# SyncE's loads and stores in a fused linear-attention and mixture-of-experts kernel, issued in program order

## The chip, the cores and the metric

The kernel runs on one core of a Trainium2 chip. A core has five engines with a queue of instructions each: TensorE (PE in the profile; its weight loads are PEld), VectorE (DVE), ScalarE (ACT), GpSimd (POOL) and SyncE (SP). SyncE does no arithmetic here: it issues the DMAs, one after the other. An instruction that waits for a semaphore holds up whatever stands behind it in its own queue.

The metric is the device time of one launch in microseconds (us). A time given for a kernel is the median of several runs. A profile is one further execution with its own time.

## The reference

Attention with an exponential feature map on 8 batches, 8 heads, 576 positions and 64 channels gives 4608 rows of 512. A mixture of experts with 8 experts then works on those rows that a gate lets through.

```python
def phi(x):
    proj = np.einsum('bhsd,df->bhsf', x, w_phi)
    proj = proj - np.max(np.abs(proj), axis=-1, keepdims=True)
    return np.concatenate([np.exp(proj), np.exp(-proj)], axis=-1)
q_p, k_p = (phi(q), phi(k))
kv = np.einsum('bhsf,bhsd->bhfd', k_p, v)
z = np.sum(k_p, axis=2)
num = np.einsum('bhsf,bhfd->bhsd', q_p, kv)
den = np.einsum('bhsf,bhf->bhs', q_p, z)[..., None] + 1e-06
x = (num / den)                      # as rows of 512
...
do_compute = x @ w_skip > 0
logits = xc @ w_gate                 # xc: the rows let through
e_idx = np.argmax(logits, axis=1)
...
h = np.maximum(xc[mask] @ w1[e], 0.0)
y[mask] = gate_w[mask, None] * (h @ w2[e])
out[do_compute] = xc + y
```

## The kernel before

**Units and steps.** Attention is cut into 16 units of keys (k) and 16 units of queries (q), each four heads of one batch: unit 2b is the first half of batch b's heads, unit 2b+1 the second. A unit has five items, i = 0 to 4, where item 0 holds the last 64 positions. The loop at L690 runs over 92 steps, numbered t in the code. Unit j of k has its items at steps 5j to 5j+4, and unit j of q six steps later (CFG "off"). At each step the stages work on items of different age (CFG "lag"): the transposition into xT or xTt at once (st_t, L264, on VectorE: L275 for item 0, L277 for items 1 and 2 together and for 3 and 4 together), the projection one step later (st_proj, L280: TensorE L289, VectorE L294 and L296), the exponentials three steps later, the products with v or with the stored state four steps later (st_use_k L346, st_use_q L420).

**What SyncE has to do in attention.** All the DMAs below are on its one queue, and these are the steps at which the program writes them down:

- raw k of unit j+1 (st_load, L243, four DMAs): step 5j. A tile "raw" has four buffers, two for k and two for q in turn, so this load can start when items 3 and 4 of k unit j-1 are transposed, at step 5j-2.
- raw q of unit j (L243, four DMAs): step 5j+1; then v of unit j (st_loadv, L253, four DMAs, two buffers): step 5j+1; then the last positions of v (st_loadvt, L262, four small DMAs, "vt"): step 5j+3.
- three stores for each batch b, kept in the list "later" and written down at the head of their step. store_half (L471, with L473 when b is odd) puts half of the rows into the scratch tensor xrows at step 16+10b; its data are ready two steps before. store_rows (L532, with L534) puts the other half there at step 21+10b, once post (L481) has worked out gate values. rest (L598, with L603 when b is odd) writes the rows to the output at step 27+10b.

Two small loads of gate weights (L115, L116) come at step 6.

**Who sets the order.** The program only writes the instructions down. A scheduler, part of the language, plans the run with its own idea of durations and puts the instructions of each engine in a fixed order; it inserts the semaphores. It prefers what was written down first, but moves an instruction ahead of others that are not ready in its plan. From step 8 to step 78 TensorE is exempt (CFG "man"): there its instructions keep the order of the program. SyncE and the other engines have the scheduler's order everywhere.

**After attention.** Two slots for the busiest experts are picked early (pick, L614) so that their weights (load_chunk, L161: SyncE L170 and L173, ScalarE L174, VectorE or GpSimd L175) can be loaded near the end of attention. Then come the expert phases (mm1, mm2), with rows gathered and results scattered by GpSimd, and a loop for overflow (L1063) that does not run here.

Of the kernel before, what the change touches and what calls it, by code (L numbers as in the profile page):

```python
# [24 lines left out]
def kernel(  # L25
# [88 lines left out]
    def setup_aug():  # L114
        nc.sync.dma_start(out=wgs[:, :, 0:E], in_=w_gate.rearrange("(g p) e -> p g e", p=P))  # L115
        nc.sync.dma_start(out=wgs[:, :, E:E + 1], in_=w_skip.rearrange("(g p o) -> p g o", p=P, o=1))  # L116
        nc.gpsimd.memset(aug, 0.0)
        for hd in range(2):
            r = slice(hd * D, (hd + 1) * D)
            c = hd * NA1  # L120
            for g in range(NP2):
                nc.gpsimd.tensor_copy(out=aug[r, g, c:c + D], in_=ident[r, hd * D:(hd + 1) * D])
            nc.gpsimd.tensor_copy(out=aug[r, :, c + D:c + NA1], in_=wgs[r])

    def setup():
        nc.gpsimd.memset(ones_b, 1.0)
        nc.gpsimd.memset(ones_f, 1.0)
        nc.gpsimd.memset(Stot, 0.0)
        nc.gpsimd.affine_select(
            out=tri, in_=ones_b, pattern=[[1, P]], base=-1, channel_multiplier=-1,  # L130
            compare_op=ALU.is_ge, fill=0.0,
        )
        nc.gpsimd.iota(iota_p, pattern=[[1, P]], base=0, channel_multiplier=0, allow_small_or_imprecise_dtypes=True)
        nc.gpsimd.iota(desc, pattern=[[-1, E]], base=E, channel_multiplier=0, allow_small_or_imprecise_dtypes=True)
        nc.gpsimd.memset(ones_b, 1.0)
        NB2 = B // 2
        kt_i = const.tile([P, 2, NT], I32, name="kt_i")
        kv_ = kt_i.rearrange("p c (b t) -> p c b t", t=9)
        nc.gpsimd.iota(kv_[:, 0, :, 0:8], pattern=[[2 * S, NB2], [512, 2], [1, 4]], base=0, channel_multiplier=4)
        nc.gpsimd.iota(kv_[:, 0, :, 8:9], pattern=[[2 * S, NB2], [1, 1]], base=1024, channel_multiplier=1)  # L140
        for q4 in range(4):
            r = slice(q4 * 32, q4 * 32 + 32)
            nc.gpsimd.iota(
                kv_[r, 1, :, 0:8], pattern=[[2 * S, NB2], [S, 2], [1, 4]], base=4 * q4, channel_multiplier=18)
            nc.gpsimd.iota(
                kv_[r, 1, :, 8:9], pattern=[[2 * S, NB2], [1, 1]], base=(q4 // 2) * S + 16 + q4 % 2, channel_multiplier=18)
        h_i = const.tile([P, 2, NT], I32, name="h_i")
        nc.vector.tensor_scalar(out=h_i[:, 1], in0=kt_i[:, 0], scalar1=127, scalar2=None, op0=ALU.bitwise_and)
        nc.vector.tensor_tensor(out=h_i[:, 0], in0=kt_i[:, 0], in1=h_i[:, 1], op=ALU.subtract)
        nc.vector.tensor_scalar(out=h_i[:, 1], in0=h_i[:, 1], scalar1=1.0, scalar2=None, op0=ALU.add)  # L150
        nc.vector.tensor_copy(out=sid, in_=kt_i[:, 1])
        nc.gpsimd.memset(ft[:, NS2:NSL, 1:2], 0)
        nc.gpsimd.memset(ft[:, NS2:NSL, 3:4], int(BIG))
        nc.vector.tensor_copy(out=ids.rearrange("p t c -> p c t"), in_=h_i)
# [48 lines left out]
    with ExitStack() as actx:  # L203
# [45 lines left out]
        def st_loadv(u):  # L249
            u.v = ld.tile([P, 4, 4 * D], F32, tag="v", name="v")  # L250
            u.vt = vts[u.g % 2]
            for q4 in range(4):
                nc.sync.dma_start(  # L253
                    out=u.v[q4 * 32:q4 * 32 + 32].rearrange("p h (t c) -> p h t c", c=D),
                    in_=vv[u.g][:, :, 4 * q4:4 * q4 + 4, :],
                )

        def st_loadvt(u):
            for pr in range(2):
                for q2 in range(2):  # L260
                    r = pr * 64 + q2 * 32
                    nc.sync.dma_start(out=u.vt[r:r + 32, pr], in_=vv[u.g][:, 2 * pr:2 * pr + 2, 16 + q2, :])  # L262
# [403 lines left out]
        def run_stage(lag, f):  # L666
            for items, us, off in streams:
                s = now[0] - off - lag
                if 0 <= s < n:
                    f(*items[s])  # L670
# [7 lines left out]
        def f_t():  # L678
            for items, us, off in streams:
                s = now[0] - off  # L680
                if s == CFG["ql"]:
                    st_load(us[0])
                if 0 <= s < n:
                    u, i = items[s]
                    st_t(u, i)
                    if i == 0 and s // 5 + 1 < len(us):
                        st_load(us[s // 5 + 1])

        man = None
        for t in range(n + OFF + LA):  # L690
            if CFG["man"] and t == CFG["man"][0]:
                man = ExitStack()
                man.enter_context(tc.manual_schedule(engines={mybir.EngineType.PE}))
            if CFG["man"] and t == CFG["man"][1]:
                man.close()
            now[0] = t
            for w, f in [x for x in later if x[0] <= t]:
                later.remove((w, f))
                f()
            for c in CFG["order"]:  # L700
                if c == "Z":
                    run_stage(LZ, st_z)
                elif c == "A":
                    run_stage(LA, st_aug)
                elif c == "U":
                    run_stage(LU, f_use)
                elif c == "E":
                    run_stage(LE, f_exp)
                elif c == "P":
                    run_stage(LP, st_proj)  # L710
                else:
                    f_t()
            run_stage(LU - 3, lambda u, i: st_loadv(u) if (i == 0 and u.kind == "k") else None)
            run_stage(CFG["vtl"], lambda u, i: st_loadvt(u) if (i == 0 and u.kind == "k") else None)
            if t == CFG["at"]:
                setup_aug()
            if t == 1:
                setup()


    pools = {}
# [378 lines left out]
```

## Time and profile before

| | |
|---|---|
| median of 3 runs (lowest, highest) | 742.93 us (741.94, 747.6) |
| the profiled execution's own time | 747.26 us |
| span from its first to its last instruction | 745.5 us |
| busy over the span: TensorE, VectorE, ScalarE, GpSimd | 616.0, 536.2, 337.8, 352.7 us |
| mean DMA rate over the span | 169 GB/s |

The trace divides into a start, in which the first units are loaded (to about 60 us), a steady part of attention (60 to 380 us), its end (380 to 446 us) and the experts (446 to 738 us). In a row of the timeline stand the start, the length, the engine, the line, the operation, what it writes and reads, the shapes, how many were merged, and in brackets how long the engine sat idle before and what ended that. "SPq" is SyncE's queue: its rows are issues of DMAs, not transfers. In the row of a group, the number behind the bar is the busy time, then the mean in ns, then the engine's idle time just before those instructions and what ended it.

### The profile page before, as it was taken

How to read it: one execution, taken by the hardware profiler on the slowest of the kernel's cores; microseconds unless marked ns; L12 is line 12 of the kernel's file. 1: busy time of each engine (PE TensorE's matmuls, PEld its weight loads, DVE VectorE, ACT ScalarE, POOL GpSimd, SP SyncE). 2: the span in 40 equal slices, each digit the busy share in tenths (PEclk: the TensorE clock that was granted, in tenths of full speed). 3: DMA queues.
4: the chain of work that ended last, by engine and by line, in shares of the span. 5: the costliest groups of instructions: out<-in, count | busy, mean ns of one | idle time of the engine just before them, and what ended most of it. 6: DMA issues, size and time to landing. Idle time of an engine off the chain costs nothing. (4 is left out here: it accounts for less than half of the span.)

```text
span 745.5 us, 16745 instructions
## 1 busy us (share of the span) xinstructions
PE 616.0 (83%) x6333; PEld 506.2 (68%) x6333; DVE 536.2 (72%) x1203; ACT 337.8 (45%) x649; POOL 352.7 (47%) x293
## 2 busy tenths in 40 slices
PE   2468879779888888898799969199989898998994
PEld 1246667657666666676577758188778787987893
DVE  3446579678677885786799769967997568558840
ACT  1224345346345543453454444314667554656520
POOL 3344336245436344362556435735576355555611
PEclk9769999989899988999899988699999899999998
DMA  9985765685487466556532746618788478786500
GB/s 192 199 172 118 163 153 154 151 205 151 102 219 172 116 190 155 149 152 149 151 96 53 211 121 206 204 39 265 224 276 269 144 251 260 235 258 210 188 16 26
DMA packets 82450, 126.03 MB, mean 169 GB/s; under 512 B 12865, under 2 KB 54977, under 8 KB 82368
## 3 DMA queue, kind: packets, MB, share of 16 engines
q1 hardware_dynamic: 79008, 115.43, 58.0%
q0 software_dynamic: 3200, 9.45, 3.9%
q8 instruction: 52, 0.85, 0.5%
q14 instruction: 30, 0.25, 0.1%
q10 hardware_dynamic: 160, 0.07, 0.1%
HBM read 101.68 MB, written 24.02 MB: 169 GB/s over the span
## 5 line engine op out<-in xcount | busy, mean ns | idle before, releaser
L321 POOL TENSOR_TENSOR z<-ek 128x512 f32<-128x512 f32 x64 | 81.3, 1272 | 176.1 <-ACT ek L313 116.9
L175 POOL TENSOR_TENSOR w<-wraw_c,w 128x1024 fp32r<-128x1024 f32 x45 | 108.9, 2435 | 77.7 <-ACT w L174 77.5
L289 PE MATMUL ps_P<-wp,xT 64*128 64x128 f32 x1024 | 91.1, 310 | 61.6 <-DVE u L296 48.2
L289 PEld LDWEIGHTS ps_P<-wp,xT 64*128 64x128 f32 x1024 | 73.1, 205 | 78.9 <-issue 50.9
L174 ACT ACTIVATE w<-wraw_c 128x1024 fp32r<-128x1024 f32 x96 | 100.5, 1057 | 51.2 <-DMA wraw_c<-in_moe_w_dram 39.0
L294 DVE TENSOR_REDUCE m<-ps_P 128x4 f32<-128x512 f32 (+1 forms) x160 | 98.6, 624 | 9.7 <-PE ps_P L289 9.6
L454 PEld LDWEIGHTS ps_O<-kva,eq 128*64 128x64 f32 x2048 | 83.3, 150 | 22.8 <-issue 8.9
L296 DVE TENSOR_TENSOR u<-ps_P,m 128x512 f32<-128x512 f32 (+1 forms) x160 | 97.0, 617 | 2.1
L454 PE MATMUL ps_O<-kva,eq 128*64 128x74 f32 x2048 | 86.9, 243 | 7.5 <-DVE acc L593 5.3
L175 DVE TENSOR_TENSOR w<-wraw_c,w 128x1024 fp32r<-128x1024 f32 x51 | 70.8, 1398 | 17.5 <-ACT w L174 17.3
L340 ACT ACTIVATE eq<-ps_U 128x512 f32<-128x512 f32 x64 | 38.0, 594 | 96.5 <-PE ps_U L334 92.2
L356 PE MATMUL ps_K<-ek,v 128*64 128x256 f32 x512 | 79.1, 433 | 0.1
L275 DVE STREAM_TRANSPOSE xTt<-raw 128x128 f32<-128x128 f32 x32 | 9.9, 310 | 91.0 <-DMA raw<-in_k_dram 57.5
L873 PE MATMUL ps_O<-w,hh 128*128 128x512 f32 x160 | 63.7, 402 | 0.3 <-ACT hh L759 0.3
L312 ACT ACTIVATE ek<-u 128x512 f32<-128x512 f32 x64 | 40.4, 631 | 42.4 <-DVE u L296 42.4
L878 PE MATMUL ps_O<-w,hlo 128*128 128x512 f32 x120 | 48.8, 408 | 3.4 <-DVE hlo L761 3.4
L334 PE MATMUL ps_U<-ident,u 128*128 128x128 f32 x288 | 50.9, 296 | 0.2 <-ACT eq L341 0.2
L801 POOL DMA_INDIRECT out_dram<-o,si x17 | 20.6, 1214 | 62.0 <-DVE o L799 50.9
L356 PEld LDWEIGHTS ps_K<-ek,v 128*64 128x64 f32 x512 | 34.1, 148 | 21.7 <-issue 8.7
L877 PE MATMUL ps_O<-w,hh 128*128 128x512 f32 x120 | 47.9, 401 | 0.0
L277 DVE STREAM_TRANSPOSE xT<-raw 128x512 f32<-128x512 f32 x64 | 44.4, 697 | 4.0 <-DMA raw<-in_k_dram 4.0
L846 PE MATMUL ps_P<-x,w 128*128 128x256 f32 x160 | 42.0, 298 | 3.5 <-DVE hlo L750 3.5
(215 smaller groups left out, 1293.3 us busy)
## 6 DMA issues: line engine op xcount, KB each, us to landing
wraw_c<-in_moe_w_dram SPq DMA_DIRECT2D x96, 512.0 KB, 4.6
raw<-in_k_dram SPq DMA_DIRECT2D x64, 280.0 KB, 5.2
raw<-in_q_dram SPq DMA_DIRECT2D x64, 280.0 KB, 8.1
v<-in_v_dram SPq DMA_DIRECT2D x64, 128.0 KB, 2.9
out_dram<-xm SPq DMA_DIRECT2D x32, 256.0 KB, 6.5
xrows<-xm SPq DMA_DIRECT2D x8, 516.0 KB, 4.8
xrows<-xm SPq DMA_DIRECT2D x8, 512.0 KB, 7.5
vt<-in_v_dram SPq DMA_DIRECT2D x64, 16.0 KB, 3.0
```

What stands on the lines that cost most here:

```text
L174: nc.scalar.activation(out=hi, in_=raw, func=AF.Copy)
L175: (eng or nc.vector).tensor_tensor(out=lo, in0=raw, in1=hi.bitcast(F32), op=ALU.subtract)
L289: nc.tensor.matmul(p[:, hd, j * NF:(j + 1) * NF], xT[r, g * P:(g + 1) * P], wp[r], start=True, stop=True)
L294: nc.vector.tensor_reduce(out=m[:, :, 0:n], in_=pv, axis=AX.X, op=ALU.max, apply_absolute_value=True)
L296: nc.vector.tensor_tensor(out=uu[:, 0:nt, :].rearrange("p (t h) f -> p h t f", h=2), in0=pv, in1=m[:, :, 0:n].rearrange("p h (t o) -> p h ...
L321: zeng.tensor_tensor(out=z, in0=e[:, 0:2, :], in1=e[:, 2:4, :], op=ALU.add)
L334: nc.tensor.transpose(t[:, tt * P:(tt + 1) * P], uu[:, tt, :], ident)
L356: nc.tensor.matmul(o[hd * 64:hd * 64 + 64, :], u.v[:, 2 * pr + hd, g * D:(g + 1) * D], u.e[i][:, 2 * j + hd, :], start=(g == 0), stop=False,)
L454: nc.tensor.matmul(ov[s * 64:s * 64 + 64, 2 * j + hd, :], e[:, half, j, hd, s * 64:s * 64 + 64], kva[:, half, 2 * pr + hd, :], start=(half ...
L873: nc.tensor.matmul(y[sub], hh[:, t], wh[:, fi, :], start=first, stop=False)
L877: nc.tensor.matmul(y[sub], hh[:, t], wl[:, fi, :], start=False, stop=False)
L878: nc.tensor.matmul(y[sub], hlo[:, t], wh[:, fi, :], start=False, stop=last)
```

## The change

A region is put around the whole step loop of attention. Within it SyncE issues its instructions in the order in which the program writes them down: each is tied behind the one before it. The other engines keep what they had (TensorE its own region from step 8 to step 78), and the scheduler still chooses where SyncE's instructions from outside the region, the experts' weight loads among them, fall between those inside. The very first load (raw k of unit 0, L664) is written down before the region. No instruction is added or taken away; since the scheduler plans all engines together, the order on the others may come out differently too.

```diff
         man = None
+
+        sman = actx.enter_context(ExitStack())
+        sman.enter_context(tc.manual_schedule(engines={mybir.EngineType.SP}))
         for t in range(n + OFF + LA):
...
             if t == 1:
                 setup()
+        sman.close()
```

## The prediction

> **What bounds the kernel now.** The table of windows comes first, then the groups and the waits of the steady part of attention.
>
> ```profile
> 60.00:380.00 320.00, 274.11 (x3729) 213.19 (x3727) 241.45 (x681) 147.49 (x338) 144.12 (x131) 0.91 0.62 154
> L275 DVE STREAM_TRANSPOSE xTt<-raw 128x128 f32<-128x128 f32 x25 | 7.8, 312 | 69.9 <-DMA raw<-in_k_dram 47.3 <-DMA raw<-in_q_dram 18.9 <-DMA vt<-in_v_dram 2.5
> PE ps_P L289 <- DVE u L296: 36.3, 19, 4.0
> ```
>
> In these 320 us VectorE is busy 241.45 us (third engine column), and ahead of one small transposition, L275, it stands idle for 69.9 us: 311.4 of 320 us are taken. It is the bound, and 22% of it is waiting for raw k and q. TensorE is busy 274.11 us and waits 36.3 us for VectorE's u. So attention goes at VectorE's pace, and what the change does to these waits is what it is worth. The timeline of VectorE shows what kind of wait it is:
>
> ```profile
> 209.22 0.16 DVE L509 TENSOR_REDUCE mx<-L 128x4 f32<-128x32 f32 x1
> 212.62 0.31 DVE L275 STREAM_TRANSPOSE xTt<-raw 128x128 f32<-128x128 f32 x1 [3.25 <-DMA raw<-in_k_dram]
> 212.86 0.65 DVE L296 TENSOR_TENSOR u<-ps_P,m 128x512 f32<-128x512 f32 x1
> ...
> 219.12 0.31 DVE L275 STREAM_TRANSPOSE xTt<-raw 128x128 f32<-128x128 f32 x1 [1.38 <-DMA raw<-in_q_dram]
> ...
> 224.40 0.69 DVE L277 STREAM_TRANSPOSE xT<-raw 128x512 f32<-128x512 f32 x1
> 213.57 0.71 PE L289 MATMUL ps_P<-wp,xT 64*128 64x128 f32 x8 [2.76 <-DVE u L296]
> 259.40 0.49 PE L289 MATMUL ps_P<-wp,xTt 64*128 64x128 f32 x4
> ```
>
> At 209.37 VectorE reaches item 0 of k unit 10 and waits 3.25 us for it; u, which TensorE wants now, stands behind, and TensorE waits 2.76 us. Yet TensorE uses that transposition only at 259.40 (L289 from xTt, counted by units). Nothing needs the load so early: the scheduler put L275 at the place where, in its plan, the load had just landed, and on the chip it lands later. The wait is the difference between planned and real landing. SyncE's timeline gives both:
>
> ```profile
> 182.28 2.77 SPq L243 DMA_DIRECT2D raw<-in_q_dram  x4
> ...
> 199.78 1.74 SPq L253 DMA_DIRECT2D v<-in_v_dram  x4
> 201.62 1.69 SPq L262 DMA_DIRECT2D vt<-in_v_dram  x2
> 204.93 1.72 SPq L243 DMA_DIRECT2D raw<-in_k_dram  x4
> 206.75 0.84 SPq L598 DMA_DIRECT2D out_dram<-xm  x2
> 207.70 3.41 SPq L243 DMA_DIRECT2D raw<-in_q_dram  x4
> 211.78 1.07 SPq L598 DMA_DIRECT2D out_dram<-xm  x2
> 214.70 0.52 SPq L532 DMA_DIRECT2D xrows<-xm  x1
> ...
> 224.76 1.74 SPq L253 DMA_DIRECT2D v<-in_v_dram  x4
> ...
> 231.63 0.52 SPq L471 DMA_DIRECT2D xrows<-xm  x1
> ```
>
> ```profile
> raw<-in_k_dram SPq DMA_DIRECT2D x64, 280.0 KB, 5.2
> raw<-in_q_dram SPq DMA_DIRECT2D x64, 280.0 KB, 8.1
> v<-in_v_dram SPq DMA_DIRECT2D x64, 128.0 KB, 2.9
> out_dram<-xm SPq DMA_DIRECT2D x32, 256.0 KB, 6.5
> xrows<-xm SPq DMA_DIRECT2D x8, 516.0 KB, 4.8
> xrows<-xm SPq DMA_DIRECT2D x8, 512.0 KB, 7.5
> vt<-in_v_dram SPq DMA_DIRECT2D x64, 16.0 KB, 3.0
> ```
>
> **The change part by part.** *The new order.* Counting issues, the rows above are k unit 10 (204.93), q unit 9 (207.70), v units 8 and 9 (199.78, 224.76), the rows of batch 2 (214.70), the half of batch 3 (231.63). By the steps at which they are written down, the new queue around here reads: rows of batch 2, q 8, v 8, vt 8, k 10 (steps 41 to 45); half of batch 3, q 9, v 9, rest of batch 2, vt 9, k 11 (46 to 50); rows of batch 3, and so on. Two stores now stand as gates: the first group cannot start before its rows are ready (214.70 before), the second not before its half (231.63). Behind the first wait 4+4+4+4 DMAs, behind the second four or eight stores more.
>
> *Do the loads still come in time?* q 8 moves from 182.28 to behind 214.70. Its items 1 and 2 were transposed at 224.40, so landing some 10 us after the gate costs nothing by itself. k 10 moves from 204.93 to about 220 (twelve issues of 0.43 us, 1.72 for four, behind the rows) for a use at 259.40, and k 11 likewise to about 240: both far ahead. v 8 moves from 199.78 to behind q 8, and it is the tight one (a rival below). For the raw loads I put the delay itself at nothing; what hides it is the distance of one unit between transposition and use, and without that each us would be a us of TensorE.
>
> By the Trainium skill, page "DMA: Bandwidth & Descriptors", section "Rules for kernel authors", a DMA is to be issued early and its semaphore waited on late, which speaks against putting loads behind stores. Here the k load is already issued some 54 us ahead of TensorE's use (204.93 to 259.40) and VectorE still waits 3.25 us, so in this trace it is the early wait that costs; by the rule alone I would add the delay of v and q, by the rows nothing.
>
> *How long the waits become.* One burst before: k (4 x 280 = 1120 KB), two outputs (512 KB), q (1120 KB). From the first issue at 204.93 the k load lands at 212.62 (7.69 us for 1120 KB), the q load at 219.12 (14.19 us for 2752 KB). A line through both: 3.23 us and 3.98 us for each 1000 KB. Planned landing: VectorE reached k's place at 209.37 (4.44 us) and q's at 217.74, of which 3.25 us was the first wait (9.56 us). A line: 0.92 us and 3.14 us for each 1000 KB. So the error, which VectorE pays, is 2.31 us and 0.84 us for each 1000 KB: 4.62 us for this burst (3.25 + 1.38 measured). The first new group has 516 + 1120 + 512 + 64 + 1120 = 3332 KB: 5.1 us. The second has 512 + 1120 + 512 + 1024 + 64 + 1120 = 4352 KB: 6.0 us. Together 11.1 us where two bursts of before have 9.25: a fifth more. Over the steady part the waits are 69.9 us in 320, that is 11.2 us in the 51.2 us of two units, so I take 13.4, which is 2.2 us more, for each of seven batches: 15.6 us. Of VectorE's wait TensorE took on 36.3 of 69.9, or 0.52; but VectorE is occupied for 97%, so up to 1.0. I take 0.8, nearer to the 97%, since a wait that is added has no slack of VectorE's to fall into: 12.5 us.
>
> The bounds: downward the waits cannot give more than TensorE's idle time, 320 - 274.11 = 46 us. Upward, if the plan charges only an issue of 0.43 us for each DMA and the 2.72 us that k had left after its last issue (4.44 - 1.72), the planned landings are 10.0 us (17 DMAs) and 11.8 us (21 DMAs), against real 16.5 and 20.6 from the first line. That is an error of 6.5 and 8.8 us, 15.3 against 9.25: 6 us a batch, 42 us in all. I stay by the two lines, since the plan gave q 9.56 us where issues alone would give 7.0 (10 DMAs): it charges more than issues.
>
> By the Trainium skill, same page, section "Anatomy of one DMA - SWDGE (gpsimd) path", a DMA of GpSimd's path takes about 2.0 us and its bytes at 436 GB/s; that would be 4.6 us for the k load, an estimate, close to the planned 4.44. The trace has 7.69, so the measurement decides; by the rule there would be no waits to lose or win at all, and the sum would be zero.
>
> *The ends.* At the start the order up to unit 2 is the same, since buffers set it. After that q 3 goes behind the half of batch 0. I put that at nothing: VectorE's waits there move, and the bounds above cover it. At the end of attention the rest of batch 6 moves behind the half of batch 7:
>
> ```profile
> 407.12 2.84 SPq L598 DMA_DIRECT2D out_dram<-xm  x4
> 430.56 0.52 SPq L471 DMA_DIRECT2D xrows<-xm  x1
> 436.60 3.90 ACT L174 ACTIVATE w<-wraw_c 128x1024 fp32r<-128x1024 f32 x4
> ```
>
> Those four stores would land some 7 us (median 6.5) after 431, about 438; if the experts' tiles reuse that buffer, the weights at 436.60 begin about 1.5 us late, else nothing. I take nothing. The weight loads stand outside the region and may keep their place. The experts' stage I leave as it is.
>
> Sum: +12 us. The profiled execution took 747.26 us (span 745.5), so its counterpart would take about 759; its own time lies 4.3 us above the median of 742.93, and against the median the forecast is **755 us**.
>
> **The rivals.** *v comes too late (slower, more).* v goes behind a gate and 1120 KB of q. For odd batches the gate opens late:
>
> ```profile
> 372.85 0.52 SPq L532 DMA_DIRECT2D xrows<-xm  x1
> 387.29 1.08 PE L356 MATMUL ps_K<-ek,v 128*64 128x256 f32 x8
> ```
>
> v 14, behind 645 KB of rows (with L534) and q, would land 3.23 + 3.98 x 2.28 = 12.3 us after 372.85, at 385.2, and is used at 387.29: 2 us to spare. It decides from a gate that opens 2 us later, and then TensorE itself waits, at L356. Three odd batches with 5 us each, with the upward bound of the waits or half of it, make 770 to 785 us. For it: the small margin. Against: the gate follows the same arithmetic as TensorE and moves with it.
>
> *The waits stay as they are (no change).* The planned order was near the program's already, there are two bursts for two units in both, and only the second group is much larger. If the plan charges large bursts properly the error stays near 11 us a batch: 743 us. That the region does not change the order is excluded: before, the k load of 204.93 stands ahead of the rows of 214.70.
>
> *The transpositions are planned later (faster).* The loads start later, so in the plan VectorE may be full when they land, and L275 falls to a place behind the real landing. For it: VectorE's own work and waits leave under 9 us free in 320, so places are few. Against: L275 was put in within 4.44 us of the issue before, wherever it landed. If half the waits go, 35 us, and TensorE gets 0.52 of that, 18 us: about 724 us. It decides once L275 is planned over 4 us behind the planned landing.
>
> **How the numbers follow.** Waits grow: 0.38, 755 us. v late or the plan blind to bursts: 0.14, 770 to 785. No change: 0.24. Faster: 0.24, 724 us and down to 700. About 1% (7.4 us) is what a measurement of this kernel tells from no change. So faster 0.24, same 0.24, slower 0.52. The range runs from 722, which leaves out the lower half of the faster case, to 785; the likeliest case alone has 750 to 768.
>
> **What would show it.** Right: the idle time ahead of L275 in the steady part rises from 69.9 us to 80 or 95, in pairs behind L532 and L471, larger behind L471, with k the later of each pair; SyncE's own waits move from L253 to L532 and L471; TensorE's wait on u grows above 36.3; the experts' stage keeps its length. The forecast is wrong if the idle time ahead of L275 falls, if L356 shows TensorE waiting for v, or if the time moves in the experts' stage.

## The result and the profile after

| | before | after |
|---|---|---|
| median of 4 runs each (lowest, highest) | 742.43 us (738.48, 747.6) | 796.5 us (794.64, 804.83) |
| ratio, 95% interval | | 1.0746 (1.0645 to 1.0847) |
| the profiled execution: time, span | 747.26, 745.5 us | 797.33, 795.6 us |

The change makes the kernel 7.5% slower. The forecast of 755 us had the direction, but the time lies outside its range of 722 to 785. First, where it went: the first matmul of the experts, in TensorE's timeline of before and then of after (start, length, engine, line).

```profile
439.07 1.09 PE L739 MATMUL ps_U<-ident,xg 128*128 128x128 f32 x8
```

```profile
488.18 1.09 PE L743 MATMUL ps_U<-ident,xg 128*128 128x128 f32 x8
```

Attention ends 49.1 us later; from there to the end of the span it is 306.4 us before and 307.4 after. So all of it is in attention. The page's rows of the engines, before and after, show which engine did more:

```profile
PE 616.0 (83%) x6333; PEld 506.2 (68%) x6333; DVE 536.2 (72%) x1203; ACT 337.8 (45%) x649; POOL 352.7 (47%) x293
```

```profile
PE 628.4 (79%) x6333; PEld 513.6 (65%) x6333; DVE 535.3 (67%) x1203; ACT 336.1 (42%) x649; POOL 353.8 (44%) x293
```

The same 6333 matmuls take 12.4 us more; the work of VectorE, ScalarE and GpSimd changes by 1.7 us at most. So VectorE must wait longer. Its waits up to the experts, before (10 to 439 us) and after (10 to 488 us): what waited for what, us in total, times, longest.

```profile
DVE xTt L275 <- DMA raw<-in_k_dram: 57.5, 15, 6.2
DVE xTt L275 <- DMA raw<-in_q_dram: 29.8, 13, 4.2
DVE m L294 <- PE ps_P L289: 9.6, 16, 2.7
DVE den L405 <- PE ps_O L433: 5.1, 2, 3.4
DVE den L405 <- PE ps_O L454: 4.5, 11, 0.8
DVE xTt L275 <- DMA vt<-in_v_dram: 2.5, 2, 1.7
DVE xTt L275 <- issue: 1.2, 1, 1.2
```

```profile
DVE xTt L275 <- DMA raw<-in_q_dram: 69.4, 16, 6.2
DVE xTt L275 <- DMA raw<-in_k_dram: 57.8, 15, 7.6
DVE m L294 <- PE ps_P L289: 11.4, 16, 3.0
DVE den L405 <- PE ps_O L454: 10.1, 12, 2.2
DVE den L405 <- PE ps_O L433: 6.0, 5, 3.2
DVE acc L593 <- PE ps_O L587: 3.6, 2, 2.3
```

Ahead of the transposition of item 0 (L275) VectorE stands 91.0 us before (57.5 + 29.8 + 2.5 + 1.2) and 127.2 after: 36.2 us more, nearly all on q. Its waits for TensorE go from 19.2 to 31.1 us, 11.9 more. Together that is 48.1 of the 49.1 us. TensorE's waits in the steady part of after (60 to 430 us) are the other end of it:

```profile
PE ps_P L289 <- DVE u L296: 46.8, 13, 6.5
PE ps_P L289 <- DVE den L405: 32.7, 16, 7.1
```

Each of the five longest waits on den (L405) ends at most 2.3 us behind the end of a wait at L275, and of the seven longest on u at most 3.1, so both rows are the same delay passed on. How one such delay looks is seen behind the gate of 226.11 us. SyncE's timeline, then VectorE's (in brackets: idle before, and what ended it):

```profile
226.11 0.52 SPq L532 DMA_DIRECT2D xrows<-xm  x1
226.68 2.55 SPq L243 DMA_DIRECT2D raw<-in_q_dram  x4
229.32 2.36 SPq L253 DMA_DIRECT2D v<-in_v_dram  x4
231.73 4.71 SPq L262 DMA_DIRECT2D vt<-in_v_dram  x4
236.63 2.50 SPq L243 DMA_DIRECT2D raw<-in_k_dram  x4
250.23 0.52 SPq L471 DMA_DIRECT2D xrows<-xm  x1
```

```profile
230.22 0.69 DVE L294 TENSOR_REDUCE m<-ps_P 128x4 f32<-128x512 f32 x1
236.23 0.31 DVE L275 STREAM_TRANSPOSE xTt<-raw 128x128 f32<-128x128 f32 x1 [5.32 <-DMA raw<-in_q_dram]
...
244.62 0.31 DVE L275 STREAM_TRANSPOSE xTt<-raw 128x128 f32<-128x128 f32 x1 [2.68 <-DMA raw<-in_k_dram]
...
260.64 0.31 DVE L275 STREAM_TRANSPOSE xTt<-raw 128x128 f32<-128x128 f32 x1 [4.66 <-DMA raw<-in_q_dram]
...
271.76 0.31 DVE L275 STREAM_TRANSPOSE xTt<-raw 128x128 f32<-128x128 f32 x1 [3.83 <-DMA raw<-in_k_dram]
```

Behind the rows (L532) stand q, v, vt and k, as the new order has it. VectorE reaches q's place at 230.91 (236.23 - 5.32), only 4.8 us behind the gate; q lands 10.1 us behind it. It reaches k's place at 241.94, and k lands at 244.62, 18.5 us behind the gate. The next two belong to the gate of 250.23. The four small vt loads take 4.71 us to issue, 1.18 each; two of before took 0.85 each (1.69). It goes with their place in the queue, not with their size: behind the gate of 250.23 the four outputs (L598) stand in that place, right behind q and v, and take 4.47 us, and the vt loads behind them 3.14. SyncE's waits over the whole run name what it waits for, first its longest of before, then after:

```profile
SPq L253 <- PE ps_K L356: 98.1, 13, 11.6
```

```profile
SPq L471 <- DVE lgm L417: 95.5, 8, 20.7
...
SPq L532 <- DVE xt L529: 67.3, 3, 23.5
SPq L532 <- DVE xm L529: 67.0, 4, 20.0
...
SPq L262 <- DMA raw<-in_q_dram: 27.9, 29, 1.5
```

SyncE's long waits stood at the loads of v before and are at the two stores now. At L262 it waits 29 times (5 before) for raw q DMAs that it has just issued, 27.9 us in all, and at L598 21 times, 20.2 us. Why it must was not tried. The consequence is in the rows: k's first issue is 10.5 us behind the gate (236.63 - 226.11).

### The profile page after: what moved, and what is told of

The parts are those of the page before. It is cut to its first block, busy times and chain, and to the rows that moved or that the text cites. A ratio compares the mean times of both kernels' runs of the same rounds, so it can differ in the third digit from the quotient of the medians.

```text
span 795.6 us, 16703 instructions
## 1 busy us (share of the span) xinstructions
PE 628.4 (79%) x6333; PEld 513.6 (65%) x6333; DVE 535.3 (67%) x1203; ACT 336.1 (42%) x649; POOL 353.8 (44%) x293
## 5 line engine op out<-in xcount | busy, mean ns | idle before, releaser
L289 PE MATMUL ps_P<-wp,xT 64*128 64x128 f32 x1024 | 96.8, 324 | 95.3 <-DVE u L296 62.8
L289 PEld LDWEIGHTS ps_P<-wp,xT 64*128 64x128 f32 x1024 | 77.9, 217 | 113.3 <-issue 92.7
L294 DVE TENSOR_REDUCE m<-ps_P 128x4 f32<-128x512 f32 (+1 forms) x160 | 98.9, 625 | 12.1 <-PE ps_P L289 11.4
L296 DVE TENSOR_TENSOR u<-ps_P,m 128x512 f32<-128x512 f32 (+1 forms) x160 | 97.6, 620 | 2.1
L454 PEld LDWEIGHTS ps_O<-kva,eq 128*64 128x64 f32 x2048 | 84.8, 152 | 17.0 <-issue 11.2
L275 DVE STREAM_TRANSPOSE xTt<-raw 128x128 f32<-128x128 f32 x32 | 9.9, 311 | 127.2 <-DMA raw<-in_q_dram 69.4
L356 PE MATMUL ps_K<-ek,v 128*64 128x256 f32 x512 | 80.2, 439 | 0.0
L334 PE MATMUL ps_U<-ident,u 128*128 128x128 f32 x288 | 51.5, 299 | 0.3 <-ACT eq L341 0.2
L356 PEld LDWEIGHTS ps_K<-ek,v 128*64 128x64 f32 x512 | 34.6, 151 | 22.2 <-issue 9.6
L277 DVE STREAM_TRANSPOSE xT<-raw 128x512 f32<-128x512 f32 x64 | 44.4, 696 | 3.8 <-DMA raw<-in_k_dram 3.8
L805 POOL DMA_INDIRECT out_dram<-o,si x17 | 18.3, 1074 | 63.1 <-DVE o L803 51.4
L836 PE MATMUL ps_P<-x,w 128*128 128x384 f32 x160 | 37.4, 354 | 9.3 <-DVE hsum L842 9.3
```

What stands on the lines that cost most here:

```text
L289: nc.tensor.matmul(p[:, hd, j * NF:(j + 1) * NF], xT[r, g * P:(g + 1) * P], wp[r], start=True, stop=True)
L294: nc.vector.tensor_reduce(out=m[:, :, 0:n], in_=pv, axis=AX.X, op=ALU.max, apply_absolute_value=True)
L296: nc.vector.tensor_tensor(out=uu[:, 0:nt, :].rearrange("p (t h) f -> p h t f", h=2), in0=pv, in1=m[:, :, 0:n].rearrange("p h (t o) -> p h ...
L334: nc.tensor.transpose(t[:, tt * P:(tt + 1) * P], uu[:, tt, :], ident)
L356: nc.tensor.matmul(o[hd * 64:hd * 64 + 64, :], u.v[:, 2 * pr + hd, g * D:(g + 1) * D], u.e[i][:, 2 * j + hd, :], start=(g == 0), stop=False,)
L454: nc.tensor.matmul(ov[s * 64:s * 64 + 64, 2 * j + hd, :], e[:, half, j, hd, s * 64:s * 64 + 64], kva[:, half, 2 * pr + hd, :], start=(half ...
```

## The experiments

The theory: SyncE's order itself costs nothing. What costs is that instructions which nobody needs yet stand early in VectorE's queue, at places where the plan has the load landed, and that the stores as gates let the loads start in bursts whose landing the plan misjudges by more. The main rival: the loads start so late that the order costs time even without those early waits. A second rival, or addition: ScalarE has the same disease at L527 (the copy of row numbers beside the rows, a buffer that the store must have left), and its share counts. All ratios are to the kernel before, run beside.

**The gates five steps later.** In the changed kernel, both stores are written down seven steps behind their data instead of two, so that the loads of those steps stand ahead of them.

```diff
-                    later.append((now[0] + 2, store_half))
+                    later.append((now[0] + 7, store_half))
...
-                later.append((now[0] + 2, store_rows))
+                later.append((now[0] + 7, store_rows))
```

> The region stays, but both stores to xrows are written down five steps later, when their data have long been ready. Theory A (the stores are gates; the loads that queue behind them go out in large bursts and land later than planned): the idle time ahead of L275 falls from 127 us over the whole run to about 90, TensorE's waits of more than 3.5 us between 60 and 430 us from 12 to about 3, and the time to 735 to 755 us. Theory B (the fixed order among the loads themselves, q then v then vt then k, is what costs): idle time ahead of L275 above 115 us, time above 780 us. Theory C (the other engines' plans came out worse): time unclear, but not tied to the idle time ahead of L275.

Measured: 752.13 us, ratio 1.0107 (1.0053 to 1.0161). The row of the group in its list:

```profile
L275 DVE STREAM_TRANSPOSE xTt<-raw 128x128 f32<-128x128 f32 x32 | 9.9, 310 | 107.3 <-DMA raw<-in_k_dram 54.4 <-DMA raw<-in_q_dram 52.9
```

The wait is 107.3 us (91.0 before, 127.2 after), and 44 of the 54 us of the loss are back. With SyncE still in the order of the program, the place of two stores is most of it. The time is as theory A had it; the wait is not, which was to fall to about 90 us.

**Only the halves five steps later.** The first of the two edits alone.

```diff
-                    later.append((now[0] + 2, store_half))
+                    later.append((now[0] + 7, store_half))
```

> The region stays, and only the first store of each batch (L471, L473) is written down five steps later; the second (L532) stays as a gate. Theory A: about half of the loss comes back, idle time ahead of L275 about 105 to 115 us, time 760 to 780 us. Theory B: no change, about 796 us.

Measured: 769.54 us, ratio 1.036 (1.0304 to 1.0415). Half of the loss is back, so either gate does harm. The waits at L275 are 122.9 us, where 105 to 115 had been expected: only 4.3 us fewer than with both gates, while the time is 27 us less. The size of these waits alone doesn't give the time. VectorE's waits for TensorE (L294, L405, L593) up to the experts are 14.9 us here and 31.1 with both gates; that is 16 us of the difference. TensorE's busy time differs too, 618.8 us here and 628.4. Its waits of more than 3.5 us, from 60 us to the experts, go with the time: 3 before, 3 with both stores late, 8 here, 13 with both gates. Why the same waits at L275 lead to fewer of them is not settled, and a worse plan of the other engines, which may change with each edit, is not excluded as a part of it.

**Item 0 transposed late, in both orders.** The wait at L275 is taken away by moving the instruction: it is tied behind VectorE's L296 of the step two before its own, so that VectorE does needed work first.

```diff
-            nc.vector.tensor_tensor(
+            u_of[now[0]] = nc.vector.tensor_tensor(
...
-                    st_t(u, i)
+                    if i == 0 and s > 5:
+                        with tc.issue_after(u_of[now[0] - 2].ins):
+                            st_t(u, i)
+                    else:
+                        st_t(u, i)
...
+        u_of = {}
```

With the order of the program on SyncE:

> The changed kernel, with L275 (item 0) tied on VectorE behind the u of two steps before, so that it is no longer planned as soon as its load has landed in the plan. If the wait is only the distance between planned and real landing of a load that nobody needs yet, the idle time ahead of L275 falls from 127 us to under 30 (the start has some 25 that stay), TensorE's long waits vanish, and the time is 690 to 720 us, below the kernel before. If the loads really come too late behind the stores, VectorE waits as long as now or TensorE waits at L289 for xTt instead, and the time stays above 770 us.

Measured: 706.92 us, ratio 0.9498 (0.9446 to 0.9551). With the scheduler's order:

> The kernel before, with the same tie of L275. If early planned transpositions are what the kernel before lost 91 us of VectorE to, that idle time falls under 30 us and the time is 690 to 715 us, within 1.5% of the changed kernel with the tie, so that the order of SyncE no longer matters. If VectorE's idle time only moves to other waits, the time stays at 735 to 750 us.

Measured: 687.01 us, ratio 0.9258 (0.9204 to 0.9312). The group's row in either, the program's order first:

```profile
L275 DVE STREAM_TRANSPOSE xTt<-raw 128x128 f32<-128x128 f32 x32 | 9.3, 293 | 7.0 <-DMA raw<-in_q_dram 4.3 <-DMA raw<-in_k_dram 2.6
```

```profile
L275 DVE STREAM_TRANSPOSE xTt<-raw 128x128 f32<-128x128 f32 x32 | 9.3, 292 | 6.8 <-DMA raw<-in_q_dram 4.3 <-DMA raw<-in_k_dram 2.6
```

120 us of waits gone is worth 90 us in the one, 84 us gone is worth 55 in the other. Both kernels were held by them, and the difference between the orders shrinks from 54 us to 20. That it would be gone, within 1.5%, did not come true. The loads of item 0 are in time: VectorE takes them late and waits for them no more. What is left in the program's order is the next such place; VectorE's waits of that kernel from 60 to 350 us have

```profile
DVE xT L277 <- DMA raw<-in_q_dram: 20.3, 5, 6.0
```

that is the transposition of the other items.

**All transpositions late, in both orders.** The condition becomes `if s > 5:`, so L277 is tied as well.

> The changed kernel with both transpositions, L275 and L277, tied behind the u of two steps before. With L275 alone tied, VectorE still waited 24 us at L277 for raw q, and 20 us were left against the kernel before with the tie. If that rest is again a transposition that is planned too early, both waits vanish and the time is 685 to 697 us. If q is really too late for TensorE behind the second store of a batch, TensorE waits at L289 for xT or VectorE at L277 as before, and the time stays at 702 to 712 us.

> The kernel before with both transpositions tied. With L275 alone tied VectorE no longer waited for raw loads in the steady part, so nothing more is to be won: 682 to 692 us. If tying L277 takes away VectorE's freedom to fill its gaps, it is slower, 692 to 705 us.

Measured: 685.3 us, ratio 0.9205 (0.9161 to 0.9249), with the program's order, and 666.0 us, 0.8973 (0.8926 to 0.902), with the scheduler's. Both gain about 21 us more, and the 20 us between them stay. In the scheduler's order no gain was expected, since from 60 to 350 us VectorE no longer waited for raw loads there. What fell in that stretch is TensorE's wait for ScalarE (L334 for L341), from 14.2 to 2.0 us, and VectorE's for TensorE (L294), from 18.2 to 4.0; why the tie does that was not shown. So the gain in the program's order, too, can't all be put down to the 20.3 us above. ScalarE's and TensorE's waits of the first, 60 to 350 us, name a candidate for those:

```profile
ACT xm L527 <- DMA out_dram<-xm: 14.2, 2, 7.1
...
PE ps_U L334 <- ACT eq L341: 19.3, 6, 5.3
```

ScalarE holds at L527 for stores, and TensorE waits for ScalarE's exponentials, which stand behind.

**L527 late, alone and with the rest.** It is tied behind the exponential of its gate values (L511), which stands ahead of it in the program.

```diff
-            nc.scalar.activation(out=ex[:, 0:nt], in_=d[:, 0:nt], func=AF.Exp)
+            exi = nc.scalar.activation(out=ex[:, 0:nt], in_=d[:, 0:nt], func=AF.Exp)
...
-                nc.scalar.activation(
-                    out=xx[:, :, DM + 1:XW], in_=sid[:, t0 + o:t0 + o + n].rearrange("p (t o) -> p t o", o=1), func=AF.Copy)
+                with tc.issue_after(exi.ins):
+                    nc.scalar.activation(
+                        out=xx[:, :, DM + 1:XW], in_=sid[:, t0 + o:t0 + o + n].rearrange("p (t o) -> p t o", o=1), func=AF.Copy)
```

Alone, on the changed kernel:

> The changed kernel, with ScalarE's small copy of row numbers into xm and xt (L527) tied behind the exponential of the same batch (L511); the transpositions stay as they are. In the changed kernel ScalarE stood idle 33 us ahead of L527 until a DMA had landed, against 7 us before. If that is a part of the loss of its own, the time falls by 10 to 25 us, to 771 to 786 us. If VectorE's waits cover it, the time stays within 6 us of 796.

Measured: 798.31 us, ratio 1.0759 (1.0695 to 1.0824), against 1.0746 for the changed kernel: nothing, although ScalarE's waits up to the experts, in the changed kernel, have

```profile
ACT xm L527 <- DMA vt<-in_v_dram: 20.8, 4, 5.9
ACT xm L527 <- DMA out_dram<-xm: 12.7, 2, 6.8
```

With the tie ScalarE waits at L527 no more. These 33.5 us lay under VectorE's waits and cost nothing as long as those are there. Together with the ties of L275 and L277, in the program's order and then in the scheduler's:

> The changed kernel with L275, L277 and L527 tied. If early planned work behind late DMAs is all that the order of SyncE costs, this is as fast as the kernel before with the transpositions tied, 664 to 674 us. If the order of the loads and stores costs something by itself, TensorE or VectorE waits for v, vt, raw or a buffer of xm, and the time stays near 685 us.

> The kernel before with L275, L277 and L527 tied. ScalarE still waited some 25 us at L527 with the transpositions tied, part of it without effect, since TensorE waited only 11 us in all in the steady part: 658 to 668 us.

Measured: 661.29 us, ratio 0.8913 (0.8838 to 0.8989), and 663.48 us, 0.8954 (0.8905 to 0.9002). The intervals overlap: with these three instructions late, the order on SyncE makes no difference, and the program's order has gained 24 us from L527 where the scheduler's had 2.5 to gain. This is what settles the main rival: the same order, with the same gates and late loads, costs nothing once these three are tied. The windows of the two from 60 to 320 us (length; then busy us and instructions of PE, PEld, DVE, ACT, POOL; granted clock; DMA share; GB/s):

```profile
60.00:320.00 260.00, 251.91 (x3721) 196.90 (x3720) 244.05 (x680) 145.69 (x340) 146.13 (x133) 1.00 0.80 188
```

```profile
60.00:320.00 260.00, 253.55 (x3749) 198.61 (x3750) 247.23 (x687) 147.29 (x343) 147.22 (x134) 1.00 0.86 192
```

TensorE is busy for 97% of it in both, and the granted clock is 1.00: it is the bound, and both versions beat both kernels by far.

**Does a long pause cost more than several short ones?** After a long wait TensorE's matmuls are slower for some microseconds (last section). To price that apart from the waits, VectorE gets work that nobody uses, on the kernel before with L275 tied (687.01 us): once every five steps one reduction of 4800 elements, or at each step one of 960.

```diff
+        pd = const.tile([P, 960], F32, name="pd")
+        pr_ = const.tile([P, 8], F32, name="pr_")
+        nc.vector.memset(pd, 0.0)
...
+            if 10 <= t < 80 and t % 5 == 0:
+                with tc.issue_after(u_of[t].ins):
+                    nc.vector.tensor_reduce(
+                        out=pr_[:, 0:5], in_=pd.rearrange("p (o f) -> p o f", o=1).broadcast_to([P, 5, 960]),
+                        axis=AX.X, op=ALU.max)
```

> The kernel before with L275 tied (687 us), plus work on VectorE that nobody uses: once every five steps one reduction of 4800 elements, about 5 us, 14 times, 70 us in all. It stands in for a wait of VectorE of 5 us. If long waits of TensorE also lower its granted clock afterwards, as the traces of before and after show behind waits of over 3.5 us, this costs more than the same work in pieces: by 14 times about 1 to 2 us, 15 to 30 us more than the next kernel, with a lower granted clock in attention. If only the sum of VectorE's time counts, both cost the same within 8 us.

> As the kernel with the 5 us pieces, but the same work in 70 pieces of 960 elements, about 1 us, one in every step. If the clock after long waits matters, this is 15 to 30 us faster than the kernel with the 5 us pieces, with few waits of TensorE above 3.5 us; if only VectorE's sum counts, the same within 8 us. VectorE has some 14% free in the steady part, so either costs less than 70 us: 25 to 60 us above 687.

Measured: 729.94 us for the blocks (ratio 0.9806, 0.9748 to 0.9864) and 742.37 us for the pieces (0.9989, 0.9958 to 1.0019). The rows of the two groups (duration least, median, most; first and last start):

```profile
L727 DVE TENSOR_REDUCE pr__132<-pd x14: 5128/5136/5147, 46.1 to 370.1; 128x5 f32<-128x4800 f32 x14
```

```profile
L727 DVE TENSOR_REDUCE pr__132<-pd x70: 1126/1135/1143, 44.4 to 405.8; 128x1 f32<-128x960 f32 x70
```

14 x 5.136 = 71.9 us of blocks cost 42.9 us, 0.60 each; 70 x 1.135 = 79.5 us of pieces cost 55.4 us, 0.70 each. The blocks were expected to cost 15 to 30 us more than the pieces; they cost 12 less. But the pieces did not leave TensorE's clock full: from 60 to 340 us the granted clock is 0.94 with the blocks and 0.93 with the pieces. They shifted the plan as well: VectorE got waits that the other does not have in this measure,

```profile
DVE xm L416 <- DMA xrows<-xm: 25.8, 6, 6.1
```

so the pair tells nothing on the price of the slow clock. It stays open.

## Why the prediction was right in kind and wrong in size

*The bound and the kind of wait: right.* VectorE's early wait at L275 holds attention, and tying that one instruction late gains 7.4% before and moves the changed kernel from 1.0746 to 0.9498.

*The stores as gates, and the loads in time: right.* SyncE waits at L532 and L471. No L356 waits for v; that rival did not happen, nor did a later planned place (the faster one). The idle time ahead of L275 in the steady part is 99.4 us (60 to 430 us), TensorE's wait for u 46.8. The start cost nothing (the first L506 below stands at 104.6 us before, 103.5 after), nor did the end: from the seventh L506 (407.2 and 456.3) to the experts it is 31.9 us in both. The experts keep their length within 1 us, as assumed.

*How long the waits become: this step failed.* It put the error at 5.1 us behind the rows and 6.0 behind the half, 13.4 us a batch in place of 11.2, so +2.2. The two groups above have 5.32 + 2.68 = 8.0 and 4.66 + 3.83 = 8.5 us. Over five batches, from one L506 to the sixth (a reduction that comes once a batch; durations, then first and last start), before and then after:

```profile
L506 DVE TENSOR_REDUCE L<-lgm x6: 629/635/642, 104.6 to 361.1; 128x36 f32<-128x288 f32 x6
```

```profile
L506 DVE TENSOR_REDUCE L<-lgm x6: 629/632/641, 103.5 to 402.9; 128x36 f32<-128x288 f32 x6
```

The groups of L275 in these stretches, again before and then after:

```profile
L275 DVE STREAM_TRANSPOSE xTt<-raw 128x128 f32<-128x128 f32 x20 | 6.2, 311 | 55.0 <-DMA raw<-in_k_dram 40.9 <-DMA raw<-in_q_dram 10.4 <-DMA vt<-in_v_dram 2.5
```

```profile
L275 DVE STREAM_TRANSPOSE xTt<-raw 128x128 f32<-128x128 f32 x20 | 6.2, 312 | 84.2 <-DMA raw<-in_q_dram 45.1 <-DMA raw<-in_k_dram 39.1
```

The waits are 11.0 us a batch before and 16.8 after: 5.8 more, not 2.2. A batch takes 51.3 us before and 59.9 after: 8.6 more, where the sum had 2.2 x 0.8 = 1.8. Two things were mis-sized. The plan is shorter than its line: behind the rows VectorE comes to k 15.8 us after the gate (241.94 - 226.11), of which 5.32 is its wait for q, so k was planned at 10.5, and the line had 11.4; behind the half it is 13.0 against 14.6. And the real landing is longer: 18.5 against 16.5 and 21.5 against 20.6. A line through one burst of k, outputs and q was asked for a queue of other make: a store in front and, between the two loads, DMAs at which SyncE itself stops. For the twelve issues between the rows and k the prediction had 0.43 us each, 5.2 in all; it was 10.5. The upward bound of the same part (the plan charges issues alone: 10.0 and 11.8 us, an error of 6.5 and 8.8) gave 6 us a batch, close to the 5.8 measured, though the parts were 8.0 and 8.5; it was in the text, and set aside since the plan had charged q 9.56 us in the one burst seen. The end of a range that rests on one sample deserved more of the weight.

*The share that TensorE takes on: failed too.* 0.8 was taken and at most 1.0 allowed. It is 49.1 / 36.2 = 1.36: more than the whole of the waits at L275. TensorE's own matmuls took 12.4 us longer besides, and VectorE waited 11.9 us more for TensorE (19.2 to 31.1). A sum that only passes a wait on had no term for that, so its ceiling of 42 us was none. That the slower matmuls made VectorE wait is inferred: where TensorE's busy time was 618.8 us (only the halves late), these waits were 14.9.

*"In pairs behind L532 and L471, larger behind L471, with k the later": right but for the size.* The waits come in such pairs, q first. In the ten pairs of those five batches the two add up to 8.6 us behind L532 and 8.2 behind L471 in the mean: not larger.

*The rule weighed there.* In the Trainium skill, page "DMA: Bandwidth & Descriptors", section "Rules for kernel authors", a DMA is issued early and waited on late. Waiting late is the half that counted: 687.01 us in place of 742.43, with SyncE still in the scheduler's order.

## What to carry to other kernels

Idle time of the bounding engine ahead of an instruction whose result is used much later is a scheduling fault of its own: tie that instruction behind work that is needed first, and only then judge the order of the DMAs. Such waits lie under one another (here, in the program's order, L275, L277, then L527), so a cure that does nothing alone can be worth 24 us once the wait above it is gone. Where a plan's mistakes set the time, a move of DMAs changes the size of the mistakes, and a line fitted to one burst says little about a burst of another composition.

## What the runs showed of the hardware

In the changed kernel a long wait leaves TensorE slower. Its timeline behind the gate of 226.11 us, and the windows there (length; busy of PE, PEld, DVE, ACT, POOL; granted clock):

```profile
230.33 1.08 PE L356 MATMUL ps_K<-ek,v 128*64 128x256 f32 x8
...
237.60 2.08 PE L289 MATMUL ps_P<-wp,xT 64*128 64x128 f32 x16 [4.45 <-DVE u L296]
239.60 1.97 PE L356 MATMUL ps_K<-ek,v 128*64 128x256 f32 x8
```

```profile
230.00:232.40 2.40, 2.40 (x49) 1.91 (x46) 0.78 (x2) 0.71 (x2) 1.79 (x2) 1.00 1.01 202
...
237.60:239.60 2.00, 2.00 (x16) 1.78 (x16) 1.90 (x15) 1.09 (x2) 0.68 (x2) 0.50 0.88 187
239.60:241.50 1.90, 1.90 (x12) 1.14 (x12) 1.90 (x4) 0.00 (x0) 1.90 (x4) 0.50 0.97 252
```

The granted clock is 1.00 ahead of the wait of 4.45 us, 0.50 for the 3.9 us behind it, and the same eight matmuls of L356 take 1.97 us in place of 1.08. By the Trainium skill, page "TensorE: Matmul & The Clock Gate", section "HAM oscillation — how this bites in real kernels", the rule is to leave TensorE no gaps over some 3.4 us; the trace agrees here, with 4.45 us, but not on 3.4 us as the limit. In the same kernel a shorter wait does it too:

```profile
273.98 2.55 PE L289 MATMUL ps_P<-wp,xT 64*128 64x128 f32 x16 [2.46 <-DVE u L296]
```

The granted clock is 1.00 ahead of these 2.46 us and 0.50 for the 4.0 us behind them; behind 2.20 us (86.67) it stays 1.00. The slow clock fits the 12.4 us by which the same matmuls grew, and their fall to 587.0 us (TensorE's busy time) in the kernel with all three instructions late. What the slow clock costs by itself, apart from the waits that bring it about, was not separated.
